# A convolution-attention and feed-forward kernel on one core: a softmax constant moved to ScalarE, the bound of x from a sum of four maxima, and VectorE's side work moved to the ends of groups of four units

## The chip, the core and the metric

The kernel runs on one core of one Trainium2 chip. The metric is the device time of one execution, in microseconds. The engines are TensorE (PE; its weight loads are PEld), VectorE (DVE), ScalarE (ACT), GpSimd (POOL) and SyncE (SP), which issues the DMAs. Each engine works off its own queue in order and waits for the others by semaphores.

## What is computed

```python
# attention: a softmax over K=7 taps weighs 7 shifted copies of x, per head
w = weight_gen - max(weight_gen, axis=-1)          # [4, 4096, 8 heads, 7 taps]
w = exp(w);  w = w / (sum(w, axis=-1) + 1e-9)
y = einsum('bshk,bskhg->bshg', w, windows_of_7(x)) # [4, 4096, 192]
# feed-forward over the 16384 rows of y
h = y @ w_in                                       # 192 -> 2048
g = h * (1 / (1 + exp(-1.702 * h)))
out = g @ w_out                                    # 2048 -> 192, float32
```

## The kernel before

The 16384 rows are cut into 32 **blocks** of 512 rows. Each block has 16 **units**, one for each 128 of the 2048 inner columns, and units are written out in **groups of four** (u0 to u3). So a block has four groups; they are called A, B, C and D here.

One unit: `whole` (L379 to L382) and `halves` (L390, L391, one pair for two units) put h into a PSUM bank, with float16 high and low parts. `gate` is a ScalarE tanh (L396) and a VectorE product (L397). `split` is a ScalarE copy of the high part (L402) and a VectorE residue (L403), the last read of the bank. `second` (L413 to L415) multiplies the parts with w_out, 12 matmuls per unit, one group later.

TensorE's order in a group is: whole u0, 12 second matmuls of an earlier unit, whole u1, the two pairs of halves, 12 seconds, whole u2, 12 seconds, whole u3, 12 seconds. VectorE's order is: gate u0, gate u1, split u0, split u1, gate u2, split u2, gate u3, split u3. The first matmul L390 of a group's halves marks its start on TensorE below.

The h banks come from a pool of five PSUM banks, `ps_h`; a new tile gets the bank that was given back longest ago.

Beside the units runs the preparation of later blocks, one step at a time:

- `softmax` (L129 to L140): VectorE max, GpSimd subtract, ScalarE exp, VectorE sum (L135), VectorE add of 1e-9 (L136), VectorE reciprocal, GpSimd multiply.
- `attend` (L146, L161): GpSimd's seven taps of a block, a multiply and (from the second tap) an add of 768 elements, into a tile `acc`, of which there are two.
- `scales`: a power-of-two scale from the largest |acc| of the block. VectorE: a reduce over acc (L224), a transpose (L198), a reduce (L199) and, against a mask `groups`, a multiply that spreads four partial maxima over four columns (L200). TensorE adds over partitions with a matrix of ones (L203, its result is the tile `top` in one of the five h banks). VectorE takes the largest of four (L205), cuts it to its exponent (L206) and forms the scales (L210 to L212, L233, L238).
- `split_x`: ScalarE (L264) and VectorE (L267, two instructions) cut acc into float16 parts; `turn` transposes them by DMA into `xt` and copies a part into `xd`, which `whole` and `halves` of that block read.

Where these steps stand is set by hand. `plan(slots, generator)` gives each step a time, counted in units, and `until(end)` inside a group lets out all steps that are due. A slot's fraction of a group, 0 to 4, picks the place: below 0.7 between gate u0 and gate u1, below 1.4 between split u0 and split u1, below 2.1 after gate u2, below 3 after gate u3, and from 3 on at the group's end, after split u3. For a block that starts at unit n, before: `scales` at n - 12.6 (end of group A of the block ahead), n - 9.9 and n - 9.7 (group B, after gate u3), `split_x` at n - 8.9 and n - 8.3 (end of group B). The max of a softmax stands at n - 40, its sum at n - 33, the end of a group A.

Of the kernel before, what the change touches and what calls it, by code (L numbers as in the profile page):

```python
# [22 lines left out]
def conv_attention_then_ffn(  # L23
# [100 lines left out]
    def softmax(blk, eng, out=None):  # L124
# [89 lines left out]
    def scales(blk):  # L214
# [241 lines left out]
    with tc.manual_schedule():  # L456
# [54 lines left out]
        plan((8.8, 11.2, 11.7), scales(1))  # L511
        plan((11.8,), scales_gate(1))
        plan((11.9,), scales_out(1))
        plan((12.2, 12.7), split_x(1))
        plan((12.9, 14.1), turn(1))
# [115 lines left out]
```

## Time and profile before

| | before |
|---|---|
| median of 3 runs | 1122.77 us (1122.59 to 1123.49) |
| profiled execution, its time | 1120.45 us |
| its span, first to last instruction | 1118.7 us |
| PE busy | 1062.0 us (95%) |
| DVE busy | 920.8 us (82%) |
| ACT busy | 708.4 us (63%) |
| POOL busy | 711.1 us (64%) |
| mean granted TensorE clock | 0.986 |

The busy shares are means over a start of some 90 us, in which weights are prepared and TensorE waits much, and a long steady part. TensorE is nearest to the span, but matmuls are pipelined, so a busy TensorE is not one at its peak; what matters is how far apart groups start.

### The profile page before, as it was taken

The numbers are of one execution on the slowest core, as the hardware profiler recorded it, in microseconds if no ns is written. First come the engines' busy times: TensorE is split into PE (matmuls) and PEld (weight loads), VectorE is DVE, ScalarE is ACT, GpSimd is POOL, SyncE is SP. The second block draws the span as 40 slices with busy tenths as digits, with TensorE's granted clock in tenths as the row PEclk, the third lists the DMA queues.
The fourth block names the chain that finished last, engine by engine and source line by source line (L and its number), as shares of the span: only waits on it lengthen the run. The fifth ranks groups of instructions, "written<-read, shape, count | busy, mean of one in ns | idle before, by whom it ended". The sixth has DMA issues, their size and how long they took to land.

```text
span 1118.7 us, 22160 instructions
## 1 busy us (share of the span) xinstructions
PE 1062.0 (95%) x8821; PEld 724.8 (65%) x8821; DVE 920.8 (82%) x1656; ACT 708.4 (63%) x1215; POOL 711.1 (64%) x483
## 2 busy tenths in 40 slices
PE   4388999999999999999999999999999999999998
PEld 4155666666666666666666666666666666666666
DVE  9887788888888888888888888888888888888765
ACT  5855666666666666666666666656666666666665
POOL 5346886666687666678666668766667866669200
PEclk8699999999999999999999999999999999999999
DMA  9301210313021021202112121121202102110110
GB/s 314 103 1 46 75 32 17 89 32 87 18 89 32 18 89 32 84 20 70 37 32 89 30 75 32 31 75 32 90 22 82 31 18 89 32 30 17 32 32 15
DMA packets 73231, 60.71 MB, mean 54 GB/s; under 512 B 60588, under 2 KB 65964, under 8 KB 71592
## 3 DMA queue, kind: packets, MB, share of 16 engines
q1 hardware_dynamic: 73128, 59.30, 18.4%
q8 instruction: 69, 1.13, 0.4%
q14 instruction: 34, 0.28, 0.1%
HBM read 31.96 MB, written 12.58 MB: 40 GB/s over the span
## 4 chain that ended last, share of the span: by engine, by line
DVE 57%; ACT 20%; PE 17%; issue 6%; DMA 0%; DVEq 0%; SPq 0%; ACTq 0%
DVE h L397 19%; DVE g L403 17%; ACT g L402 15%; DVE wm L136 4%; DVE tf L200 3%; ACT th L396 3%; PE o L413 3%; DVE xs L267 3%; PE o L415 3%; PE o L414 3%; DVE top L224 2%; PE h L379 2%; PE h L380 2%; PE h L381 2%; PE h L382 2%
## 5 line engine op out<-in xcount | busy, mean ns | idle before, releaser
L402 ACT ACTIVATE g<-h 128x512 f16<-128x512 f32 x512 | 305.2, 596 | 330.7 <-DVE h L397 330.7
L413 PE MATMUL o<-wos,g 128*128 128x192 f16 x2048 | 505.4, 247 | 0.0
L415 PE MATMUL o<-woh,g 128*128 128x192 f16 x2048 | 504.1, 246 | 0.0
L414 PE MATMUL o<-wol,g 128*128 128x192 f16 x2048 | 504.1, 246 | 0.0
L403 DVE SCALAR_TENSOR_TENSOR g<-g,h 128x512 f16<-128x512 f16 x512 | 345.1, 685 | 158.5 <-ACT g L402 147.8
L396 ACT ACTIVATE th<-h,s 128x512 f32<-128x512 f32 x512 | 336.3, 682 | 56.0 <-PE h L391 54.3
L397 DVE SCALAR_TENSOR_TENSOR h<-th,h 128x512 f32<-128x512 f32 x512 | 343.1, 687 | 17.7 <-ACT th L396 17.4
L161 POOL TENSOR_TENSOR acc<-acc,prod 128x768 f32<-128x768 f32 x186 | 337.1, 1813 | 14.6
L146 POOL TENSOR_TENSOR prod<-xb,wb 128x768 f32<-128x768 f32 x186 | 287.6, 1546 | 9.8
L413 PEld LDWEIGHTS <-g 128*128 128x128 f16 x2048 | 200.2, 98 | 102.4 <-issue 57.1
L414 PEld LDWEIGHTS <-g 128*128 128x128 f16 x2048 | 200.5, 98 | 41.1 <-issue 0.3
L379 PE MATMUL h<-xt,w0l 128*128 128x512 f16 x512 | 195.3, 381 | 18.8 <-DVE g L403 13.2
L415 PEld LDWEIGHTS <-g 128*128 128x128 f16 x2048 | 200.5, 98 | 0.0
L380 PE MATMUL h<-xt,w0h 128*128 128x512 f16 x512 | 194.9, 381 | 0.0
L381 PE MATMUL h<-xt,w0h 128*128 128x512 f16 x512 | 194.8, 380 | 0.0
L382 PE MATMUL h<-xt,wth 128*128 128x512 f16 x512 | 194.6, 380 | 0.0
L131 POOL TENSOR_TENSOR wb<-wb,wm 128x224 f32<-128x224 f32 x31 | 17.9, 577 | 263.6 <-DVE wm L129 263.6
L381 PEld LDWEIGHTS <-w0h 128*128 128x128 f16 x512 | 50.3, 98 | 61.0 <-issue 1.1
L382 PEld LDWEIGHTS <-wth 128*128 128x128 f16 x512 | 50.3, 98 | 61.0 <-issue 1.0
L391 PE MATMUL h<-xd,tl 64*128 64x512 f16 x256 | 81.7, 381 | 1.8 <-DVE g L403 1.8
L390 PE MATMUL h<-xt,tl 64*128 64x512 f16 x256 | 77.1, 381 | 0.0
L379 PEld LDWEIGHTS <-w0l 128*128 128x128 f16 x512 | 50.2, 98 | 26.6 <-DVE g L403 19.0
(89 smaller groups left out, 595.3 us busy)
## 6 DMA issues: line engine op xcount, KB each, us to landing
xb<-in_x_dram SPq DMA_DIRECT2D x12, 1344.0 KB, 6.3
out_dram<-osb SPq DMA_DIRECT2D x31, 384.0 KB, 2.4
wb<-in_weight_gen_dram SPq DMA_DIRECT2D x16, 224.0 KB, 3.1
ro<-in_moe_w_out_dram SPq DMA_DIRECT2D x4, 768.0 KB, 12.1
xb<-in_x_dram SPq DMA_DIRECT2D x3, 768.0 KB, 6.3
ri<-in_moe_w_in_dram SPq DMA_DIRECT2D x4, 512.0 KB, 8.3
xb<-in_x_dram SPq DMA_DIRECT2D x4, 504.0 KB, 5.8
xd<-xt SPq DMA_DIRECT2D x31, 64.0 KB, 2.1
```

Of the source, the lines that this page charges most:

```text
L146: eng.tensor_tensor(to.rearrange("p j (h g) -> p (j h) g", g=G), xv, wv, ALU.mult)
L161: nc.gpsimd.tensor_tensor(acc, acc, t, ALU.add)
L379: nc.tensor.matmul(ps, lhsT=w0l[:, s], rhs=x0, start=start, stop=False)
L381: nc.tensor.matmul(ps, lhsT=w0h[:, s], rhs=x0, start=False, stop=False)
L382: nc.tensor.matmul(ps, lhsT=th_[:, s], rhs=x1, start=False, stop=stop)
L396: nc.scalar.activation(t, hp[u], AF.Tanh, scale=scale[u[0]][:, 4:5])
L397: nc.vector.scalar_tensor_tensor(hp[u], t, 1.0, hp[u], ALU.add, ALU.mult)
L402: nc.scalar.activation(g[:, 0], hp[u], AF.Copy, scale=2.0**-12)
L403: nc.vector.scalar_tensor_tensor(g[:, 1], g[:, 0], -(2.0**12), hp.pop(u), ALU.mult, ALU.add)
L413: nc.tensor.matmul(o, lhsT=lo, rhs=wos[:, d], start=a and j % 2 == 0, stop=False, skip_group_check=True)
L414: nc.tensor.matmul(o, lhsT=hi, rhs=wol[:, d], start=False, stop=False, skip_group_check=True)
L415: nc.tensor.matmul(o, lhsT=hi, rhs=woh[:, d], start=False, stop=z, skip_group_check=True)
```

## The change

Three edits.

1. In `softmax`, for blocks 2 and up, the 1e-9 is added by a ScalarE Copy with a bias, in the same step as the sum; the reciprocal becomes a step of its own, later.
2. In `scales`, the second reduce writes straight into the column that goes to TensorE; the multiply with `groups` goes. The matmul with ones then yields the sum of four partial maxima (each of 32 partitions) instead of four maxima, and the reduce over four (L205) goes too; the exponent is cut from PSUM directly. The sum is at most four times the largest. The bounds of the weights keep the old form.
3. The slots move.

```diff
         nc.vector.tensor_reduce(m, w, axis=AX.X, op=ALU.add)
-        nc.vector.tensor_scalar(m, m, 1e-9, None, ALU.add)
+        if blk < XB:
+            nc.vector.tensor_scalar(m, m, 1e-9, None, ALU.add)
+        else:
+            nc.scalar.activation(m, m, AF.Copy, bias=1e-9)
+            yield
         nc.vector.reciprocal(r, m)
...
+        n = 4 if exact else 1
         nc.vector.transpose(a, t)
-        nc.vector.tensor_reduce(m[:, 0:1], a, axis=AX.X, op=ALU.max)
-        nc.vector.tensor_scalar(four, groups, m[:, 0:1], None, ALU.mult)
+        if exact:
+            nc.vector.tensor_reduce(m[:, 0:1], a, axis=AX.X, op=ALU.max)
+            nc.vector.tensor_scalar(four, groups, m[:, 0:1], None, ALU.mult)
+        else:
+            nc.vector.tensor_reduce(four[:, 0:1], a, axis=AX.X, op=ALU.max)
         yield
...
-        nc.vector.tensor_reduce(m[:, 1:2], ps[:, 0:4], axis=AX.X, op=ALU.max)
-        nc.vector.tensor_scalar(e, m[:, 1:2].bitcast(I32), 0x7F800000, None, ALU.bitwise_and)
+        top = ps[:, 0:1]
+        if exact:
+            top = m[:, 1:2]
+            nc.vector.tensor_reduce(top, ps[:, 0:4], axis=AX.X, op=ALU.max)
+        nc.vector.tensor_scalar(e, top.bitcast(I32), 0x7F800000, None, ALU.bitwise_and)
...
-            plan([n - 12.6, n - 9.9, n - 9.7], scales(blk))
+            plan([n - 12.2, n - 10.4, n - 10.3], scales(blk))
-            plan([n - 8.9, n - 8.3], split_x(blk))
+            plan([n - 9.5, n - 8.2], split_x(blk))
```

VectorE, end of a group A and the group B behind it, before (`tf` is the column or columns for TensorE, `ta` the transposed maxima, `wm` and `wr` a softmax's sum and reciprocal):

```order
L403 SCALAR_TENSOR_TENSOR g<-g,h 128x512
L224 TENSOR_REDUCE top_102<-acc 128x1
L198 STREAM_TRANSPOSE ta<-top_102 128x32
L199 TENSOR_REDUCE tm<-ta 128x1
L200 TENSOR_SCALAR tf<-groups,tm 128x4
L397 SCALAR_TENSOR_TENSOR h<-th,h 128x512 x2
L403 SCALAR_TENSOR_TENSOR g<-g,h 128x512 x2
L397 SCALAR_TENSOR_TENSOR h<-th,h 128x512
L403 SCALAR_TENSOR_TENSOR g<-g,h 128x512
L397 SCALAR_TENSOR_TENSOR h<-th,h 128x512
L205 TENSOR_REDUCE tm<-top 128x1
L206 TENSOR_SCALAR s<-tm 128x1
```

The same place after:

```order
L414 SCALAR_TENSOR_TENSOR g<-g,h 128x512
L135 TENSOR_REDUCE wm<-wb 128x32
L235 TENSOR_REDUCE top_103<-acc 128x1
L203 STREAM_TRANSPOSE ta<-top_103 128x32
L208 TENSOR_REDUCE tf<-ta 128x1
L408 SCALAR_TENSOR_TENSOR h<-th,h 128x512 x2
L414 SCALAR_TENSOR_TENSOR g<-g,h 128x512 x2
L408 SCALAR_TENSOR_TENSOR h<-th,h 128x512
L217 TENSOR_SCALAR s<-top 128x1
```

The multiply into `tf` and the reduce of `top` are gone, the sum of a softmax has joined the end of group A, and the scale's instructions stand behind gate u2 where they stood behind gate u3.

TensorE in group B, before (`h_2786` is the bank of u3):

```order
L381 MATMUL h_2786<-xt_2434,w0h_94 128x512
L382 LDWEIGHTS wth_96
L382 MATMUL h_2786<-xt_2434,wth_96 128x512
L203 LDWEIGHTS ones_92
L203 MATMUL top_2847<-tf_2757,ones_92 128x4
L413 LDWEIGHTS g_2750
```

and after (`h_2779` is the bank of u2):

```order
L392 MATMUL h_2779<-xt_2429,w0h_94 128x512
L393 LDWEIGHTS wth_96
L393 MATMUL h_2779<-xt_2429,wth_96 128x512
L211 LDWEIGHTS ones_92
L211 MATMUL top_2819<-tf_2752,ones_92 128x1
L424 LDWEIGHTS g_2719
```

The matmul with ones now stands one unit earlier on TensorE, ahead of 12 seconds and u3's four matmuls.

VectorE in block 0, where block 1 is prepared, before (the two L267 stand in group D behind split u0):

```order
L397 SCALAR_TENSOR_TENSOR h<-th,h 128x512 x2
L403 SCALAR_TENSOR_TENSOR g<-g,h 128x512
L267 SCALAR_TENSOR_TENSOR xs<-acc,s,xs 128x4x128
L267 SCALAR_TENSOR_TENSOR xs<-acc,s,xs 128x4x64
L403 SCALAR_TENSOR_TENSOR g<-g,h 128x512
```

and after (end of group C, ahead of group D's first two gates):

```order
L414 SCALAR_TENSOR_TENSOR g<-g,h 128x512
L135 TENSOR_REDUCE wm<-wb 128x32
L129 TENSOR_REDUCE wm<-wb 128x32
L278 SCALAR_TENSOR_TENSOR xs<-acc,s,xs 128x4x128
L278 SCALAR_TENSOR_TENSOR xs<-acc,s,xs 128x4x64
L408 SCALAR_TENSOR_TENSOR h<-th,h 128x512 x2
```

The DMA that turns block 1 follows the two instructions, so it is issued ahead of group D's gates and no longer behind its split u0. On GpSimd the subtract of a softmax, before between the third and fourth tap of a block, now stands between its fifth and sixth, and waits for a max at the end of a group C (before: in the group C, behind gate u0). The order of SyncE's DMAs is the same.

## Rows read from the trace of the kernel before

**Rows 1.** Windows: stretch, each engine's busy us (instructions), granted clock, DMA share, GB/s

```profile
91.40:188.16 96.76, 96.76 (x821) 66.78 (x821) 77.17 (x145) 63.71 (x108) 70.08 (x48) 1.00 0.16 44
188.16:1049.18 861.02, 847.85 (x7100) 577.31 (x7100) 722.26 (x1273) 547.10 (x935) 595.90 (x393) 1.00 0.18 49
```

**Rows 2.** Timeline of PE, group B of block 6 and C's start: start, us, instruction

```profile
261.86 0.39 PE L390 MATMUL h<-xt,tl 64*128 64x512 f16 x1
...
264.25 0.25 PE L413 MATMUL o<-wos,g 128*128 128x192 f16 x1
...
266.11 0.17 PE L203 MATMUL top<-tf,ones 128*128 128x4 bf16 x1
...
267.81 0.39 PE L379 MATMUL h<-xt,w0l 128*128 128x512 f16 x1 [0.52 <-DVE g L403]
...
270.63 0.39 PE L390 MATMUL h<-xt,tl 64*128 64x512 f16 x1
...
271.03 0.37 PE L391 MATMUL h<-xd,tl 64*128 64x512 f16 x1
```

**Rows 3.** Timeline of DVE over groups A and B of the same block

```profile
256.46 1.26 DVE L397 SCALAR_TENSOR_TENSOR h<-th,h 128x512 f32<-128x512 f32 x2
...
262.91 0.94 DVE L224 TENSOR_REDUCE top<-acc 128x1 f32<-128x768 f32 x1
...
264.36 1.45 DVE L200 TENSOR_SCALAR tf<-groups,tm 128x4 bf16<-128x4 f32 x1
265.72 1.28 DVE L397 SCALAR_TENSOR_TENSOR h<-th,h 128x512 f32<-128x512 f32 x2
267.06 1.29 DVE L403 SCALAR_TENSOR_TENSOR g<-g,h 128x512 f16<-128x512 f16 x2
...
272.61 1.14 DVE L267 SCALAR_TENSOR_TENSOR xs<-acc,s,xs 128x512 f16<-128x512 f32 x2
```

**Rows 4.** Timeline of POOL over the same stretch

```profile
263.97 1.81 POOL L161 TENSOR_TENSOR acc<-acc,prod 128x768 f32<-128x768 f32 x1
274.72 0.57 POOL L131 TENSOR_TENSOR wb<-wb,wm 128x224 f32<-128x224 f32 x1 [8.95 <-DVE wm L129]
```

**Rows 5.** DVE groups by line in 220.69 to 1015.54: busy us, mean ns, idle before

```profile
L136 DVE TENSOR_SCALAR wm<-wm 128x32 f32<-128x32 f32 x24 | 43.2, 1799 | 0.8
L200 DVE TENSOR_SCALAR tf<-groups,tm 128x4 bf16<-128x4 f32 x24 | 34.7, 1446 | 0.9
...
L135 DVE TENSOR_REDUCE wm<-wb 128x32 f32<-128x224 f32 x24 | 9.1, 378 | 0.0
...
L199 DVE TENSOR_REDUCE tm<-ta 128x1 f32<-128x32 f32 x24 | 4.5, 186 | 0.8
```

**Rows 6.** ACT groups by line over the whole span

```profile
L133 ACT ACTIVATE wb<-wb 128x224 f32<-128x224 f32 x32 | 12.2, 382 | 0.7 <-POOL wb L131 0.6 <-DVE wb L131 0.2
...
L325 ACT ACTIVATION_READ_ACCUMULATOR abs<-ro 128x1 f32 x6 | 1.1, 188 | 0.0
```

**Rows 7.** Timelines of POOL, DVE, SP and PE, end of block 0, block 1's start

```profile
75.63 1.81 POOL L161 TENSOR_TENSOR acc<-acc,prod 128x768 f32<-128x768 f32 x1
77.02 0.21 DVE L233 TENSOR_SCALAR s<-s,sc 128x1 f32<-128x1 f32 x1
79.13 1.81 POOL L161 TENSOR_TENSOR acc<-acc,prod 128x768 f32<-128x768 f32 x1
79.58 3.60 DVE L267 SCALAR_TENSOR_TENSOR xs<-acc,s,xs 128x512 f16<-128x512 f32 x2
81.02 1.87 POOL L146 TENSOR_TENSOR prod<-xb,wb 128x768 f32<-128x768 f32 x1
83.24 1.55 SPq L273 DMA_TRANSPOSE xt<-xs  x1
87.03 0.61 PE L379 MATMUL h<-xt,w0l 128*128 128x512 f16 x1 [5.62 <-DMA xt<-xs]
91.40 0.39 PE L390 MATMUL h<-xt,tl 64*128 64x512 f16 x1
92.60 0.69 DVE L397 SCALAR_TENSOR_TENSOR h<-th,h 128x512 f32<-128x512 f32 x1 [3.83 <-ACT th L396]
```

More of the change, by code (lines that the diff above doesn't have):

```diff
@@ L190, in conv_attention_then_ffn, with top_of @@
     to_in, to_out = sc[:, 2:3], sc[:, 3:4]
-    def top_of(t, e):
+    def top_of(t, e, exact):
         a = spool.tile([P, 32], F32, tag="ta", name="ta", bufs=2)
@@ L197, in top_of @@
         four = spool.tile([P, 4], BF16, tag="tf", name="tf", bufs=2)
+        n = 4 if exact else 1
         nc.vector.transpose(a, t)
-        nc.vector.tensor_reduce(m[:, 0:1], a, axis=AX.X, op=ALU.max)
-        nc.vector.tensor_scalar(four, groups, m[:, 0:1], None, ALU.mult)
+        if exact:
[3 more added lines that the diff above has]
+            nc.vector.tensor_reduce(four[:, 0:1], a, axis=AX.X, op=ALU.max)
         yield
         ps = ps_h.tile([P, N], F32, tag="h", name="top")
-        nc.tensor.matmul(ps[:, 0:4], lhsT=ones, rhs=four, start=True, stop=True)
+        nc.tensor.matmul(ps[:, 0:n], lhsT=ones, rhs=four[:, 0:n], start=True, stop=True)
         yield
-        nc.vector.tensor_reduce(m[:, 1:2], ps[:, 0:4], axis=AX.X, op=ALU.max)
-        nc.vector.tensor_scalar(e, m[:, 1:2].bitcast(I32), 0x7F800000, None, ALU.bitwise_and)
+        top = ps[:, 0:1]
[3 more added lines that the diff above has]
+        nc.vector.tensor_scalar(e, top.bitcast(I32), 0x7F800000, None, ALU.bitwise_and)
     def power(e, to, inv, top):
@@ L227, in scales @@
         e = s[:, 0:1].bitcast(I32)
-        yield from top_of(t, e)
+        yield from top_of(t, e, False)
         power(e, s[:, 2:3], s[:, 3:4], 263)
@@ L328, in bound @@
         nc.vector.tensor_reduce(tops[1][:, 0:1], sums[:, a0:a1], axis=AX.X, op=ALU.max)
-        yield from top_of(tops[1], e)
+        yield from top_of(tops[1], e, True)
     def bound_in():
@@ L510, in conv_attention_then_ffn @@
         plan((8.0,), scales_out(0))
[L511 to L515, printed above, removed]
+        plan((8.2, 9.6, 9.7), scales(1))
+        plan((9.75,), scales_gate(1))
+        plan((9.8,), scales_out(1))
+        plan((10.5, 11.8), split_x(1))
+        plan((11.85, 14), turn(1))
         for blk in range(2, NB):
             n = blk * NF
-            plan([n - 12.6, n - 9.9, n - 9.7], scales(blk))
-            plan([n - 9.6], scales_gate(blk))
-            plan([n - 9.5], scales_out(blk))
-            plan([n - 8.9, n - 8.3], split_x(blk))
-            plan([n - 8.2, n - 5.8], turn(blk))
+            plan([n - 12.2, n - 10.4, n - 10.3], scales(blk))
+            plan([n - 10.25], scales_gate(blk))
+            plan([n - 10.2], scales_out(blk))
+            plan([n - 9.5, n - 8.2], split_x(blk))
+            plan([n - 8.15, n - 6], turn(blk))
             if blk == 2:
-                plan((4.8, 4.81, 8.1, 8.8, 9.1), softmax(blk, G_))
+                plan((4.8, 4.81, 8.1, 8.5, 8.8, 9.1), softmax(blk, G_))
                 plan([9.2 + 1.5 * k for k in range(K)], attend(blk))
-            else:
-                plan([n - 40, n - 39.9, n - 35, n - 33, n - 30.4], softmax(blk, G_))
-                first_tap, step = (n - 27.8, 2) if blk == 3 else (n - 30, 2.2)
-                plan([first_tap + step * k for k in range(K)], attend(blk))
+            elif blk == 3:
+                plan((3.7, 7.75, 7.8, 11.7, 13.7, 17.6), softmax(blk, G_))
+                plan([n - 27.8 + 2 * k for k in range(K)], attend(blk))
+            else:
+                plan([n - 52.3, n - 52.2, n - 48.2, n - 44.3, n - 36.3, n - 30.4], softmax(blk, G_))
+                plan([n - 30 + 2.2 * k for k in range(K)], attend(blk))
             if blk % XB == 0 and blk > XB:
```

## The prediction, made before the changed kernel ran

> **What bounds the kernel now.** I read the windows first, cut where blocks start on TensorE. Blocks 1 to 3 take 96.76 us, 32.25 each, and TensorE is busy in all of it at a granted clock of 1.00. The 26 blocks behind them take 861.02 us, 33.12 each, at the same clock and with 13.2 us of idle TensorE [rows 1]. The work is the same, so 32.25 is what TensorE itself needs for a block, 8.06 per group, and 861.02 - 26 x 32.25 = 22.5 us are lost to waits. That is the prize.
>
> Where it goes shows in one block's timeline of TensorE. Group B starts at 261.86, group C at 270.63, 8.77 later, and not 8.06. The row at 267.81 names the wait: the first matmul of C's u0 stood 0.52 us idle until a split (L403) on VectorE. The second halves of C come at 271.03, another 0.15 late [rows 2]. Together this is the 0.87 per block.
>
> Why the split is late: VectorE had finished group A at 262.9, then took 1.45 us for the multiply L200, four columns wide. So gate u0 of B started at 265.72 and its two first splits at 267.06; the first ends 0.69 later, at 267.75, and TensorE goes on at 267.81 [rows 2, 3]. L200 ends at 265.81, when GpSimd's add of a tap ends: 263.97 + 1.81 = 265.78 [rows 4]. It is not computing, it waits for GpSimd. The reduce L199 just ahead (0.19) runs under the same add and does not wait. Over 24 blocks L200 takes 1446 ns every time and the add of 1e-9, L136, 1799, against 186 and 378 for reduces of like size [rows 5].
>
> One thing makes group B the sore one: `top` takes the fifth h bank there, so C's u0 needs the bank of B's u0, four units back and not five.
>
> **The change part by part.**
>
> *The sum of maxima* takes L200 and L205 off VectorE: 1.45 + 0.15 per block. What fills `tf` now is a reduce; I price it as L199, 0.19, which it replaces, so nothing is added.
>
> *The constant on ScalarE* takes 1.80 off VectorE per block [rows 5], but not off the path: group A, in which it sat, shows no loss. The new ScalarE Copy of 32 elements lies between the 188 ns of an accumulator read and the 382 of the exp of 224 elements [rows 6]; I take 0.25. A wait comes with it: on ScalarE the next group's two tanh are queued behind it, and VectorE's gates behind those.
>
> *The moves.* I lay the new order out for a steady block, in us from each group's start on TensorE. The first gate can start 1.2 in (91.40 to 92.60) [rows 7]. From there to the end of split u3 is 6.5 (256.46 to 262.9) [rows 3]. So VectorE's main work of a group ends at 7.7 and the next begins at 8.06 + 1.2 = 9.26: 1.5 us are free at every group's end.
>
> - End of A: sum 0.38 and L224 to L199, 1.45 (262.91 to 264.36) [rows 3, 5]: 1.8. B's first gate is 0.3 late. The ScalarE add ends at 7.7 + 0.38 + 0.25 = 8.35, or 8.5 at the upper price; the tanh behind it needs its halves and cannot start before 9.26 - 0.7 = 8.56. Cost nothing. If VectorE were late here by over 0.2, the tanh would be late by the rest.
> - `tf` is ready at 7.7 + 1.8 = 9.5, 1.45 into B. TensorE now reaches the matmul for `top` behind u2, at 264.25 - 261.86 = 2.39, not at 4.25 [rows 2]. Margin 0.9; what is queued behind it on TensorE is all the rest, so past that margin each us costs one.
> - The six scale instructions, 0.15 to 0.21 each, some 1.0 in all, stand behind gate u2, where VectorE waits some 0.65 for a ScalarE copy anyway: 0.35 late. The same cost stood behind gate u3 before.
> - C's u0 is reached 267.81 - 0.69 - 261.86 = 5.26 into B. B's split u0 now ends at 1.5 + 1.34 + 0.69 = 3.5. Margin 1.7, and the loss of 0.87 is gone.
> - End of B: 1.2 + 0.3 + 6.5 + 0.35 = 8.35, then the two L267, 1.14 when GpSimd is quiet [rows 3]: 9.5, C's first gate 0.25 late. The transposing DMA leaves here, with two groups to land in; it took 3.8 [rows 7].
> - End of C: reciprocal and max, 0.7 of the 1.5 free. End of D: an exp on ScalarE.
>
> So every group should start 8.06 after the last one. **22.5 us** go; the upper end of the remaining loss is among the rivals.
>
> *GpSimd under the new order.* Its subtract waits for the max at the end of C, so a cycle starts some 0.8 behind that. It works 33.12 - 8.95 = 24.2 us of a block, less a short wait of about 0.5 [rows 4], and is done 24.3 to 25 after C's end. Three groups, 24.2, lie between an end of C and the next end of B. So the L267 pair starts just as GpSimd's last add of the cycle ends, maybe under its last 0.1 to 0.8 us. In block 0 such a pair met a busy GpSimd throughout and took 3.60 in place of 1.14 [rows 3, 7]. The page "GPSIMD Engine Reference" of the Trainium skill (Key points) says that GpSimd's SBUF interfaces are shared with VectorE instructions in a 2-port mode or with two SBUF inputs; L267 has two, L200 and L136 would be of the first kind, and the rows agree. By that rule alone the new place of L267 speaks against the change.
>
> *Block 0* has a second prize. The last VectorE part of block 1's x ended at 83.2 there; its transpose was issued at 83.24, and TensorE stood 5.62 us until 87.03 [rows 7]; from there to the halves at 91.40 took 4.37 where 32.25-us blocks need 2.8, 1.56 more. With the pair at the end of C, I put its end near 78.7: three gates and splits sooner, but tanh u1 of C now waits behind the ScalarE add (0.9) and the pair still meets GpSimd. Transposed 3.8 later, at 82.5; TensorE, which now waits some 1.9 for `top` in C, wants it at 82.3. Block 1 could start up to 5.9 sooner. Part goes back at once: block 2's seven taps begin at some 72 as before, take 24.5 with two softmax steps between (seven taps at 3.5, 79.13 - 75.63), and end near 96.5, but block 1's end of A would now be at 93. VectorE stands till 96.5 in its reduce, TensorE till 98.2 for `top`, where it would have been at 101.85 before: 3.65 sooner. Two collisions of L267 with GpSimd in blocks 1 and 2 take some 0.8. Net **2.8**, bounds 0 and 5.9. Ahead of block 0 the same two VectorE instructions go once: 0 to 1.5 (an L200 and an L205), I take **0.5**, as ScalarE and DMAs bound part of that stretch.
>
> Sum: 22.5 + 2.8 + 0.5 = 25.8. The profiled execution took 1120.45, 1.75 more than its span of 1118.7; it would become 1094.7. The median lies 2.3 above that execution, so 1122.8 - 25.8 = **1097.0**.
>
> **The rivals.**
>
> 1. *L267 collides in full in each block* (pair 3.6 or more). C's first gate starts 8.35 + 3.6 - 8.06 = 3.9 into C, its split u2 ends 4.6 later at 8.5, and D's second halves want that bank at 8.28: 0.2 lost per block. If both instructions met a fresh add, 4.5: 1.1 lost. Over 27 blocks 5 to 30 us back; mid 13, so 1110, at most 1122 or so. For it: GpSimd's end falls on the pair's start. Against: behind that add GpSimd has nothing to do for 8 us, so only the rest of one instruction can be in the way.
> 2. *The new reduce into `tf` waits for GpSimd as L200 did* (1.25 more). `tf` is then ready 2.7 into B, TensorE stands 0.3 per block: some 8 us back, 1105. Against: L199 never waited.
> 3. *The scale's small instructions wait*, slower than before. They ran while GpSimd was idle; after gate u2 of B its taps run. L210 to L212, L233 and L238 are scalar operations on SBUF as L200 is, five in a row, each of which could wait for an instruction of 1.54 to 1.81. Split u2 of B would end at 6.5 + d, and C wants its bank at 8.28. For d = 2.6 (two of five meet one) 0.85 is lost per block and the gain is gone; from there on it is slower: for d = 4.3, 2.5 lost, 27 x 2.5 = 68 us back, 1165. Against: at 77.02 L233 took 0.21 under the add that ran from 75.63 to 77.44 [rows 7], with the others around it. "VectorE: DVE Perf Modes" of the Trainium skill (the perf-mode tier table) lets tensor_scalar on float32 in SBUF use both ports, with no word on one element; that page would have them wait, and the row says no.
> 4. *The banks were not what held TensorE* and the loss comes back elsewhere: 1120 to 1125. Against: blocks 1 to 3 run at 32.25.
>
> **How the numbers follow.** Forecast 0.67, rival 1 0.15 (most of it faster, 0.02 at no change), rival 2 and other partial gains 0.07, rival 3 0.07, rival 4 0.04. About 0.2%, 2.2 us, can be told from no change. Faster 0.87, the same 0.06, slower 0.07. The range runs from 22.5 + 5.9 + 1.5 with a little of the spread of runs, 1092, up into the milder half of rival 1, 1110.
>
> **What would show it.** Groups start 8.06 apart in all blocks from 2 on, and TensorE has no idle time there for L403. L200 and L136 are gone, save for the start, and nothing on VectorE takes 1.4 us for a few elements. The L267 pair takes 1.1 to 1.9. The ScalarE add takes about 0.25 and no tanh waits for it in steady blocks. TensorE's wait for `xt` in block 0 shrinks to under 2 us, and a wait for `top` of about 2 us appears in blocks 0 and 1. Wrong if the matmul for `top` waits in every block, or if L210 to L238 grow.

## The result and the profile after

The changed kernel takes 1094.91 us (median of 4 runs, 1093.89 to 1095.54) beside 1122.68 us (1121.38 to 1123.49) before, a ratio of 0.9753 with an interval of 0.9736 to 0.977. The forecast was 1097.0 with a range of 1092 to 1110. The profiled execution took 1095.54 us with a span of 1093.6; the span of before was 1118.7, so 25.1 us of it are gone.

In the new code all lines lie further down: the halves are L401 and L402, tanh L407, gate L408, ScalarE copy L413, split L414, seconds L424 to L426, the matmul for `top` L211, the reduces into it L235 and L208, the scale's instructions L217 to L249, the two `split_x` instructions L278, the new ScalarE add L139.

The windows, cut at starts of blocks on TensorE as in [rows 1] (stretch, its length, each engine's busy us and instructions, granted clock, DMA share, GB/s): blocks 2 and 3, and the 26 blocks behind them.

```profile
120.96:185.47 64.51, 64.51 (x548) 44.53 (x548) 51.75 (x93) 43.37 (x76) 50.82 (x33) 1.00 0.18 53
185.47:1024.12 838.65, 838.65 (x7100) 578.70 (x7100) 640.74 (x1192) 558.75 (x959) 592.93 (x392) 1.00 0.18 51
```

The same 26 blocks took 861.02 us before; they now take 838.65, 32.25 or 32.26 each but for one of 32.32, and TensorE is idle in none of it. That is 22.37 us. Block 2 starts at 120.96 where it started at 123.65, 2.69 sooner. 22.37 + 2.69 = 25.06 is the whole difference of the spans.

TensorE in group B of a steady block, and the start of C, as in [rows 2]:

```profile
258.03 0.39 PE L401 MATMUL h<-xt,tl 64*128 64x512 f16 x1
...
260.43 0.17 PE L211 MATMUL top<-tf,ones 128*128 128x1 bf16 x1
...
263.30 0.38 PE L390 MATMUL h<-xt,w0l 128*128 128x512 f16 x1
...
266.11 0.39 PE L401 MATMUL h<-xt,tl 64*128 64x512 f16 x1
```

Group B is 8.08 long instead of 8.77. The matmul for `top` waits for nothing, and C's first `whole` at 263.30, 5.27 into the group, has no wait beside it; in [rows 2] it came 5.95 in and stood for a split.

VectorE over the same stretch, as in [rows 3]; a bracket gives the idle time ahead and what ended it:

```profile
251.18 1.29 DVE L408 SCALAR_TENSOR_TENSOR h<-th,h 128x512 f32<-128x512 f32 x2 [1.50 <-ACT th L407]
...
257.66 0.38 DVE L135 TENSOR_REDUCE wm<-wb 128x32 f32<-128x224 f32 x1
...
259.18 0.19 DVE L208 TENSOR_REDUCE tf<-ta 128x1 bf16<-128x32 f32 x1
259.28 1.28 DVE L408 SCALAR_TENSOR_TENSOR h<-th,h 128x512 f32<-128x512 f32 x2
...
262.43 0.15 DVE L217 TENSOR_SCALAR s<-top 128x1 int32<-128x1 int32 x1
...
263.31 0.20 DVE L249 TENSOR_SCALAR s<-s,sc 128x1 f32<-128x1 f32 x1
...
265.98 1.14 DVE L278 SCALAR_TENSOR_TENSOR xs<-acc,s,xs 128x512 f16<-128x512 f32 x2
267.32 1.29 DVE L408 SCALAR_TENSOR_TENSOR h<-th,h 128x512 f32<-128x512 f32 x2 [0.20 <-ACT th L407]
...
275.38 1.29 DVE L408 SCALAR_TENSOR_TENSOR h<-th,h 128x512 f32<-128x512 f32 x2 [0.99 <-ACT th L407]
```

and GpSimd's timeline and ScalarE's beside it:

```profile
262.38 1.55 POOL L150 TENSOR_TENSOR prod<-xb,wb 128x768 f32<-128x768 f32 x1
264.00 1.81 POOL L165 TENSOR_TENSOR acc<-acc,prod 128x768 f32<-128x768 f32 x1
```

```profile
258.07 0.23 ACT L139 ACTIVATE wm<-wm 128x32 f32<-128x32 f32 x1 [1.05 <-DVE wm L135]
258.52 1.27 ACT L407 ACTIVATE th<-h,s 128x512 f32<-128x512 f32 x2 [0.22 <-PE h L402]
```

What to see: VectorE now waits for a tanh ahead of the first gates of C, D and A (0.20, 0.99, 1.50), 2.69 us per block. The tanh waits for TensorE's halves. Over the whole span "ScalarE's tanh waits for TensorE's halves" has grown from 54.3 to 128.8 us, and "VectorE's gate waits for the tanh" from 17.4 to 82.9. The small instructions L217 to L249 take 0.15 to 0.21 while GpSimd multiplies a tap (262.38 to 263.93), and the L278 pair starts at 265.98, 0.17 behind the end of GpSimd's last add (264.00 + 1.81).

The plainest sign is the part of the page on the chain of work that ended last (shares of the span). Before:

```profile
DVE 57%; ACT 20%; PE 17%; issue 6%; DMA 0%; DVEq 0%; SPq 0%; ACTq 0%
```

and after:

```profile
PE 92%; DVE 3%; POOL 2%; ACT 2%; issue 1%; DMA 0%; POOLq 0%; ACTq 0%
```

Before, the end hung on VectorE and ScalarE; now it hangs on TensorE. The prediction did not use that line. It should have, as the experiments show.

### The profile page after: what moved, and what is told of

Its sections match the earlier page's. It is cut to its first block, busy times and chain, and to the rows that moved or that the text cites. A ratio compares the mean times of both kernels' runs of the same rounds, so it can differ in the third digit from the quotient of the medians.

```text
span 1093.6 us, 22203 instructions
## 1 busy us (share of the span) xinstructions
PE 1053.7 (96%) x8821; PEld 726.0 (66%) x8821; DVE 834.6 (76%) x1562; ACT 721.3 (66%) x1245; POOL 711.2 (65%) x483
## 4 chain that ended last, share of the span: by engine, by line
PE 92%; DVE 3%; POOL 2%; ACT 2%; issue 1%; DMA 0%; POOLq 0%; ACTq 0%
PE o L424 16%; PE o L426 15%; PE o L425 15%; PE h L391 10%; PE h L392 10%; PE h L390 10%; PE h L393 10%; PE h L401 6%; POOL acc L165 1%; POOL prod L150 1%; PE tr L183 1%; DVE h L408 1%; ACT abs L336 1%; DVE g L414 0%; ACT bits L326 0%
## 5 line engine op out<-in xcount | busy, mean ns | idle before, releaser
L424 PE MATMUL o<-wos,g 128*128 128x192 f16 x2048 | 504.9, 247 | 0.0
L426 PE MATMUL o<-woh,g 128*128 128x192 f16 x2048 | 503.7, 246 | 0.0
L414 DVE SCALAR_TENSOR_TENSOR g<-g,h 128x512 f16<-128x512 f16 x512 | 340.1, 684 | 155.3 <-ACT g L413 147.0
L413 ACT ACTIVATE g<-h 128x512 f16<-128x512 f32 x512 | 305.7, 597 | 190.8 <-DVE h L408 190.7
L407 ACT ACTIVATE th<-h,s 128x512 f32<-128x512 f32 x512 | 337.0, 683 | 128.8 <-PE h L402 128.8
L408 DVE SCALAR_TENSOR_TENSOR h<-th,h 128x512 f32<-128x512 f32 x512 | 341.8, 690 | 82.9 <-ACT th L407 82.9
L424 PEld LDWEIGHTS <-g 128*128 128x128 f16 x2048 | 200.0, 98 | 97.6 <-issue 53.0
L426 PEld LDWEIGHTS <-g 128*128 128x128 f16 x2048 | 200.3, 98 | 0.0
L402 PE MATMUL h<-xd,tl 64*128 64x512 f16 x256 | 77.7, 383 | 1.0 <-DVE g L414 1.0
L401 PE MATMUL h<-xt,tl 64*128 64x512 f16 x256 | 77.4, 383 | 0.0
```

The source lines that it names most:

```text
L407: nc.scalar.activation(t, hp[u], AF.Tanh, scale=scale[u[0]][:, 4:5])
L408: nc.vector.scalar_tensor_tensor(hp[u], t, 1.0, hp[u], ALU.add, ALU.mult)
L413: nc.scalar.activation(g[:, 0], hp[u], AF.Copy, scale=2.0**-12)
L414: nc.vector.scalar_tensor_tensor(g[:, 1], g[:, 0], -(2.0**12), hp.pop(u), ALU.mult, ALU.add)
L424: nc.tensor.matmul(o, lhsT=lo, rhs=wos[:, d], start=a and j % 2 == 0, stop=False, skip_group_check=True)
L426: nc.tensor.matmul(o, lhsT=hi, rhs=woh[:, d], start=False, stop=z, skip_group_check=True)
```

## The experiments

Each time stands beside runs of the kernel before on the same chip.

**One half of the change alone.** The first kernel is the one of before with the sum of four maxima only (no L200, no L205), all slots and the constant as they were:

```diff
-        nc.vector.tensor_reduce(m[:, 0:1], a, axis=AX.X, op=ALU.max)
-        nc.vector.tensor_scalar(four, groups, m[:, 0:1], None, ALU.mult)
+        if exact:
+            nc.vector.tensor_reduce(m[:, 0:1], a, axis=AX.X, op=ALU.max)
+            nc.vector.tensor_scalar(four, groups, m[:, 0:1], None, ALU.mult)
+        else:
+            nc.vector.tensor_reduce(four[:, 0:1], a, axis=AX.X, op=ALU.max)
...
```

> The kernel before with the sum of four maxima alone; L136 and all slots as before. Theory (two waits of VectorE for GpSimd, at the add of 1e-9 and at the multiply into tf, add up to 2.7 us of lateness of group B's first gate, against a bank margin of 1.7 us, so either one removed is enough): gate u0 of B starts about 2.5 us into B, its first split ends at 4.5, C's first matmul is reached at 5.26, no wait; steady blocks take 32.25 us and not 33.12, block 0 stays as it was: about 1100 us. Rival (the lateness is only pushed along, each us of VectorE costs): about half the loss stays, 1108 to 1112.

The second is the one of before with the constant on ScalarE only:

```diff
-        nc.vector.tensor_scalar(m, m, 1e-9, None, ALU.add)
+        if blk < XB:
+            nc.vector.tensor_scalar(m, m, 1e-9, None, ALU.add)
+        else:
+            nc.scalar.activation(m, m, AF.Copy, bias=1e-9)
+            yield
...
-                plan([n - 40, n - 39.9, n - 35, n - 33, n - 30.4], softmax(blk, G_))
+                plan([n - 40, n - 39.9, n - 35, n - 33, n - 32.9, n - 30.4], softmax(blk, G_))
```

> The kernel before with the constant on ScalarE alone; the multiply into tf and all slots as before, the reciprocal right behind the sum. Theory: the wait of 1.4 us at the end of group D goes, so A ends sooner and B's first gate starts 1.5 to 2.0 us into B although the multiply still waits for GpSimd: no wait at C, 32.25 us per block, about 1100 us. Rival (the prediction's reading, the add is off the path and only the multiply counts): no change, 1121 to 1123 us.

Measured: 1098.92 us, ratio 0.979 (0.9776 to 0.9805), and 1100.55 us, ratio 0.9806 (0.9792 to 0.9821). A window over 26 blocks from the start of block 2, first of the one, then of the other:

```profile
123.27:961.86 838.59, 838.59 (x7101) 578.46 (x7100) 656.82 (x1223) 550.88 (x936) 597.24 (x396) 1.00 0.19 53
```

```profile
126.15:964.74 838.59, 838.59 (x7100) 578.40 (x7100) 670.26 (x1249) 557.10 (x962) 596.76 (x396) 1.00 0.19 53
```

Both are at 32.25 us per block: **either half alone brings all of the steady blocks' gain.** The two do not add. This falls on the prediction's sentence that the 1.80 of L136 is "off the path"; had that been so, the second kernel would have stayed at 33.12. And the wait of the instruction that was kept shrinks as well. In the first kernel's window L136 takes 485 ns, in the second's the multiply into `tf` (there L204) takes 1034, against 1799 and 1446 in [rows 5] (groups of VectorE by line: busy us, mean ns, idle before):

```profile
L136 DVE TENSOR_SCALAR wm<-wm 128x32 f32<-128x32 f32 x26 | 12.6, 485 | 0.9
```

```profile
L204 DVE TENSOR_SCALAR tf<-groups,tm 128x4 bf16<-128x4 f32 x26 | 26.9, 1034 | 0.9
```

The price of waiting out a GpSimd instruction is in most rows what is left of it when VectorE arrives, and this shifts when anything else does: in the second kernel the same multiply takes from 0.23 to 1.64 us from one block to the next.

**The bank.** The prediction named the bank that `top` takes in `ps_h` as what makes group B sore. This kernel is the one of before with `top` in another PSUM pool from block 2 on:

```diff
-        ps = ps_h.tile([P, N], F32, tag="h", name="top")
+        ps = ps_o.tile([P, N], F32, tag="o", name="top") if other else ps_h.tile([P, N], F32, tag="h", name="top")
...
```

> The kernel before with one edit: from block 2 on, top takes a bank of the other PSUM pool, the one of the output sums, so the five h banks are not shifted in group B. All VectorE work and its waits stay. Theory (C's u0 waits because top has taken the fifth bank and it needs the bank of B's u0): C's u0 no longer waits though L200 still takes 1.4 us; only C's second halves may wait 0.2: 1101 to 1106 us. Rival (VectorE's lateness holds TensorE whatever the banks): 1121 to 1123 us.

Measured: 1122.07 us, ratio 0.9997 (0.9988 to 1.0007), no change. TensorE's starts of groups A, B and C of a block (D begins at 278.38, the next A at 286.63):

```profile
253.51 0.39 PE L390 MATMUL h<-xt,tl 64*128 64x512 f16 x1
...
261.57 0.39 PE L390 MATMUL h<-xt,tl 64*128 64x512 f16 x1
...
269.95 0.39 PE L390 MATMUL h<-xt,tl 64*128 64x512 f16 x1
```

The groups take 8.06, 8.38, 8.43 and 8.25 where they took 8.06, 8.77, 8.22 and 8.06. The sore group is gone, and the sum stays: 33.12 either way. The 26 blocks of [rows 1] in this kernel,

```profile
188.28:1049.11 860.83, 859.29 (x7100) 578.87 (x7100) 721.68 (x1273) 544.98 (x935) 595.62 (x393) 1.00 0.18 49
```

take as long as the 861.02 of before, and TensorE is busy in all but 1.54 of it, where it was idle for 13.2. So its busy time did not tell that it was held back; the spacing of groups did. The bank only chose the place at which the loss was seen. This theory fell.

**What takes its place: VectorE's own chain.** VectorE's gates and splits of a group, with the ScalarE copies in between, take 6.48 us if nothing else comes (251.18 to 257.66 above), 25.92 per block. In the kernel before, the side work came on top with no time to spare. The end of a group D in VectorE's timeline:

```profile
253.95 0.38 DVE L135 TENSOR_REDUCE wm<-wb 128x32 f32<-128x224 f32 x1
254.36 1.79 DVE L136 TENSOR_SCALAR wm<-wm 128x32 f32<-128x32 f32 x1
256.19 0.35 DVE L137 RECIPROCAL wr<-wm 128x32 f32<-128x32 f32 x1
```

From 253.95 to A's gates at 256.46 [rows 3] are 2.51 us. (The text ahead of the prediction puts this sum at the end of a group A; the rows show it at the end of a group D, one group earlier.) The end of A, 262.91 to 265.72 [rows 3], is 2.81. The L267 pair takes 1.06 (272.61 to 273.67), and the other ends of groups in this block are these:

```profile
273.67 0.69 DVE L397 SCALAR_TENSOR_TENSOR h<-th,h 128x512 f32<-128x512 f32 x1
...
280.43 1.29 DVE L397 SCALAR_TENSOR_TENSOR h<-th,h 128x512 f32<-128x512 f32 x2
...
287.06 0.38 DVE L135 TENSOR_REDUCE wm<-wb 128x32 f32<-128x224 f32 x1
```

So the gates and splits take 6.45 in A, 6.89 in B, among them the scale's instructions, 6.76 in C, among them the max, and 6.63 in D. 2.51 + 6.45 + 2.81 + 6.89 + 1.06 + 6.76 + 6.63 = 33.11, the 33.12 of a block. That the pieces of a timeline add up to its period would hold for any engine; what matters is which waits are in them. VectorE's groups by line over the 24 blocks of [rows 5] (busy us, mean ns, idle before and what ended it):

```profile
L403 DVE SCALAR_TENSOR_TENSOR g<-g,h 128x512 f16<-128x512 f16 x385 | 259.9, 685 | 120.5 <-ACT g L402 112.0
L397 DVE SCALAR_TENSOR_TENSOR h<-th,h 128x512 f32<-128x512 f32 x384 | 257.1, 686 | 0.0
```

VectorE waited for ScalarE's copies of its own products, and no gate waited for a tanh; TensorE waited for VectorE, through whichever bank came late first. The trace of before holds one more sign of this. At the start of blocks 1, 2 and 3, where TensorE lost nothing, L136 took 0.36, 0.49 and 0.72 us, and L200 in them 0.23, 0.61 and 1.44, so at most 2.16 together. From block 5 on they took 1.80 and 1.45, 3.25 together, and TensorE lost 0.87: up to 2.38 would have fitted.

After the change the same sum is 25.92 + 1.62 (257.66 to 259.28) + 0.22 + 1.14 + 0.59 = 29.5, and 32.25 - 29.5 = 2.75 is, to 0.06, the 2.69 of waits seen above. This can be tested: side work that fits into 2.69 us must cost nothing, and more must cost the difference. So reduces that nobody reads were put at the end of every group C of the changed kernel, two in one kernel and four (`range(4)`) in the other:

```diff
+        idle = spool.tile([P, 1], F32, tag="idle", name="idle", bufs=1)
+        def extra():
+            for _ in range(2):
+                nc.vector.tensor_reduce(idle, woh[:, 0:768], axis=AX.X, op=ALU.max)
+        for blk in range(2, NB):
+            plan([blk * NF - 4.1], once(extra))
```

> The changed kernel, and at the end of every group C from block 1 on two more VectorE reductions of 768 elements to a tile that nobody reads, at the price of the 768-element reduction of the changed kernel (0.94 us) 1.9 us per block. Theory (VectorE's chain of a block bounds it): the chain of the changed kernel is 29.6 of the 32.25 us that TensorE takes, idle 0.20, 0.99 and 1.50 us ahead of three of the four pairs of gates; 1.9 us fits, block stays 32.25, total 1094 to 1097. Rival (a place near the group's start is what matters, whatever the block's sum): each block loses at that place 1.9 less the 0.99 that stands behind it, some 0.9 us, 23 us in all: 1116 to 1120.

> The changed kernel, and at the end of every group C from block 1 on four more VectorE reductions of 768 elements, 3.8 us per block. Theory: the chain becomes 29.6 + 3.8 = 33.4 us, 1.1 us over TensorE's 32.25; over 26 blocks 29 us, total 1118 to 1128, TensorE idle at the starts of groups, and the last chain of waits mostly on VectorE again as in the kernel before. Rival (a place near the group's start is what matters): the loss is 3.8 less 0.99 at that place, some 2.8 us per block, 73 us: 1160 to 1170.

Measured with two: 1096.17 us, ratio 0.9759 (0.9743 to 0.9775), steady blocks at 32.25; only blocks 2, 3, 28 and 29 took more, 32.40 to 32.83. The interval overlaps that of the changed kernel nearly in full. With four: 1130.21 us, ratio 1.0065 (1.0044 to 1.0086). The chain and a window over 23 steady blocks with four:

```profile
DVE 58%; ACT 21%; PE 11%; issue 7%; POOL 2%; DMA 0%; ACTq 0%; POOLq 0%
```

```profile
240.03:1007.35 767.32, 756.28 (x6281) 510.14 (x6281) 643.55 (x1150) 489.51 (x852) 524.53 (x348) 1.00 0.18 50
```

767.32 / 23 = 33.36 per block; the four reduces took 3.90 together, 3.80 of it until the next instruction could start, and 32.25 - 2.69 + 3.80 is 33.36. The total missed its range by 2 us on the high side: 1.11 x 26 is the 29 us that were expected, and blocks 1 and 2 lost more than that, 2.1 us in block 1, whose group D took 10.12, and 3.1 in block 2 beyond its 1.11. The chain's shares are close to those of the kernel before. This is the strongest run of the study: the slack read from three brackets of one timeline gave the price of a load to a tenth of a microsecond per block.

**The second limit: `top` stands in TensorE's queue.** Here the change's slots are kept and one or both old computations put back. Both first:

```diff
-        if blk < XB:
-            nc.vector.tensor_scalar(m, m, 1e-9, None, ALU.add)
-        else:
-            nc.scalar.activation(m, m, AF.Copy, bias=1e-9)
+        nc.vector.tensor_scalar(m, m, 1e-9, None, ALU.add)
+        if blk >= XB:
             yield
...
-        if exact:
-            nc.vector.tensor_reduce(m[:, 0:1], a, axis=AX.X, op=ALU.max)
-            nc.vector.tensor_scalar(four, groups, m[:, 0:1], None, ALU.mult)
-        else:
-            nc.vector.tensor_reduce(four[:, 0:1], a, axis=AX.X, op=ALU.max)
+        nc.vector.tensor_reduce(m[:, 0:1], a, axis=AX.X, op=ALU.max)
+        nc.vector.tensor_scalar(four, groups, m[:, 0:1], None, ALU.mult)
...
```

> The changed kernel with both old computations put back (add of 1e-9 and multiply into tf on VectorE, reduce of four): only the slots are new. Theory: both waits for GpSimd now fall on the end of group A, one behind the other, so tf is ready 3.5 to 4.5 us into B while TensorE reaches the matmul for top 2.4 us in and stands 1 to 2 us in each block: 25 to 55 us over the changed kernel, 1120 to 1150 us. Rival (the moves are what freed the time): 1095 to 1100 us.

Measured: 1127.49 us (1124.91 to 1130.87), ratio 1.0058 (1.0038 to 1.0078), slower than before by 0.6%: the slots without the two edits lose. TensorE's timeline in a group B, and VectorE's groups by line over 21 steady blocks (698.62 us, 33.27 each):

```profile
267.49 0.18 PE L205 MATMUL top<-tf,ones 128*128 128x4 bf16 x1 [0.75 <-DVE tf L202]
```

```profile
L136 DVE TENSOR_SCALAR wm<-wm 128x32 f32<-128x32 f32 x21 | 33.7, 1607 | 0.7
...
L202 DVE TENSOR_SCALAR tf<-groups,tm 128x4 bf16<-128x4 f32 x21 | 7.1, 338 | 0.8
```

Now L136 stands at the end of A and waits out the add, and the multiply behind it, L202, finds GpSimd between two instructions in 19 of the 21 blocks: 0.25 us there and 1.17 in the other two, 0.34 in the mean, instead of 1.45. By the sum of VectorE's chain (29.5 + 1.61 + 0.34 + 0.19 for the reduce of four) 31.6 would fit into 32.25. It doesn't help, since `tf` comes late: group B takes 9.0, the others 8.06. In the changed kernel `tf` is ready at 259.37 and TensorE reaches the matmul at 260.43, a margin of 1.06; L136 and L202 put 1.95 in front of it, 0.9 too much.

The constant alone put back,

```diff
-        if blk < XB:
-            nc.vector.tensor_scalar(m, m, 1e-9, None, ALU.add)
-        else:
-            nc.scalar.activation(m, m, AF.Copy, bias=1e-9)
+        nc.vector.tensor_scalar(m, m, 1e-9, None, ALU.add)
+        if blk >= XB:
             yield
```

> The changed kernel with the add of 1e-9 back on VectorE, in the step of the sum at the end of group A. Theory (with the first four runs: VectorE's and ScalarE's chain of one block took 33.1 us and bounded the kernel before; the new order has room there, but TensorE stands for top whenever tf is later than 2.4 us into B): the add starts about 258.0 in the traced block and waits for GpSimd's add to end at 258.8, so tf is ready about 2.2 us into B, at the edge: 0 to 0.4 us lost per block, 1095 to 1106 us. Rival (the ScalarE add is what gained): 1110 us or more.

and the old maxima alone put back (the second piece of the diff above),

> The changed kernel with the old maxima: the multiply into tf and the reduce of four back on VectorE, the constant on ScalarE, the new slots. Theory: the multiply starts 1.35 us into B and waits for a GpSimd instruction that ends 2.4 into B, so TensorE stands 0 to 0.4 us per block for top: 1095 to 1106 us. Rival (the sum of maxima is what gained): 1110 us or more.

give 1106.88 us (1105.12 to 1108.14), ratio 0.986 (0.9844 to 0.9876), 0.9 us beyond its range, and 1105.02 us, ratio 0.9845 (0.9829 to 0.9862). In the first of them, over 22 steady blocks:

```profile
266.67:987.96 721.29, 713.41 (x6007) 487.82 (x6007) 569.14 (x1034) 468.54 (x793) 501.08 (x333) 1.00 0.18 50
```

32.79 per block in the mean. One block of them takes 34.36, with an L136 of 3.90 that ends behind two further GpSimd instructions; nearly all others take 32.71, with an L136 of 1.42: 1.42 - 1.06 = 0.36 against 0.46 measured. "TensorE's `top` waits for VectorE's `tf`" comes 26 times. In the second the multiply takes 0.28 and 1.2 us in turn, and 2.1 to 2.6 in three blocks; a steady group B takes 8.08 or 8.3 with it, 9.2 to 9.7 in those three, and the one of block 1 takes 13.46. So in the old slots either edit was enough, and **in the new slots both are needed for the full gain**: the new slots have moved the limit from VectorE's sum to one date, `tf` at 2.4 us into group B.

**What the slots bring.** Both new computations in the kernel of before, with its old slots (the diffs of the first two kernels together):

> The constant on ScalarE and the sum of maxima, all slots as before (the reciprocal right behind the sum). Theory: steady blocks at 32.25 us, nothing more than either of the two alone gives, since TensorE bounds then; block 0 as before with its wait of 5.6 us for the transposed x: 1098 to 1101 us. Rival (the two gains add up): 1080 us or less.

and the changed kernel with block 1's slots alone set back:

```diff
-        plan((8.2, 9.6, 9.7), scales(1))
+        plan((8.8, 11.2, 11.7), scales(1))
...
-        plan((10.5, 11.8), split_x(1))
-        plan((11.85, 14), turn(1))
+        plan((12.2, 12.7), split_x(1))
+        plan((12.9, 14.1), turn(1))
```

> The changed kernel with block 1's preparation at its old slots; all else new. Theory: steady blocks as in the changed kernel, but block 0 waits about 5.6 us for the transposed x again and block 1 no longer about 2 us for top: block 2 starts 2.5 to 3 us later, 1097 to 1099 us. Rival (the start's difference is the granted clock or the spread of runs): 1094 to 1096 us.

Measured: 1097.89 us, ratio 0.9782 (0.9768 to 0.9797), and 1099.15 us, ratio 0.9791 (0.9776 to 0.9806). Each total lies 0.1 to 0.2 us beyond its range, the first below, the second above. Steady blocks take 32.25 in both. Block 2 starts at 123.15 in the one, at 124.76 in the other, and at 120.96 in the changed kernel. So the slots of the steady blocks bring nothing, and those of block 1 bring some 2 to 4 us, once; the first interval still touches that of the changed kernel, the second does not.

**Two tries at the start.** What is left to gain lies in blocks 0 and 1. In the changed kernel, TensorE waits in block 0 for `top` and for block 1's transposed x, and in block 1 for `top` (timeline of TensorE; compare the 5.62 in [rows 7]):

```profile
70.24 0.18 PE L211 MATMUL top<-tf,ones 128*128 128x1 bf16 x1 [1.64 <-DVE tf L208]
83.77 0.39 PE L390 MATMUL h<-xt,w0l 128*128 128x512 f16 x1 [0.46 <-DMA xt<-xs]
99.16 0.18 PE L211 MATMUL top<-tf,ones 128*128 128x1 bf16 x1 [1.94 <-DVE tf L208]
```

The first try plans block 2's softmax and taps much sooner:

```diff
-        if blk < XB:
+        if blk <= XB:
             nc.vector.tensor_scalar(m, m, 1e-9, None, ALU.add)
...
-        plan((8.2, 9.6, 9.7), scales(1))
+        plan((7.9, 9.6, 9.7), scales(1))
...
-        plan((10.5, 11.8), split_x(1))
-        plan((11.85, 14), turn(1))
+        plan((10.5, 11.6), split_x(1))
+        plan((11.65, 14), turn(1))
...
-                plan((4.8, 4.81, 8.1, 8.5, 8.8, 9.1), softmax(blk, G_))
-                plan([9.2 + 1.5 * k for k in range(K)], attend(blk))
+                plan((3.6, 3.65, 4.81, 5.3, 5.5), softmax(blk, G_))
+                plan((5.6, 7.0, 8.4, 9.8, 12.2, 13.2, 14.2), attend(blk))
...
-                plan((3.7, 7.75, 7.8, 11.7, 13.7, 17.6), softmax(blk, G_))
+                plan((3.7, 3.75, 7.8, 11.7, 13.7, 17.6), softmax(blk, G_))
```

> The changed kernel with only its first blocks planned otherwise: block 1's scales, x parts and transposes a little sooner in block 0, block 2's softmax and attention some five units sooner, block 2's constant on VectorE. In the changed kernel block 1 begins at 86.60 us and its group B then waits about two microseconds for the number that the sum of block 2's attention gives. Theory (VectorE's chain bounds a block, and what is left over the steady blocks is in the order of the first two): block 1 begins near 85.3, its group B no longer waits, and the total falls by 2 to 4 us, to about 1091.5 (1090 to 1093). Rival: the sooner work lies in the same gaps of VectorE and the transposing DMA lands no sooner, so block 0 gives back what block 1 gains: 1094 to 1096.

Measured: 1099.01 us, ratio 0.9786 (0.9771 to 0.9802), slower than the changed kernel. Block 1 no longer waits (32.25), but begins at 91.69 in place of 86.60. VectorE's timeline in block 0, where it still converts w_out (L359, L377), and GpSimd's beside it:

```profile
60.61 0.74 DVE L359 SCALAR_TENSOR_TENSOR wol<-ro,sc,woh 128x512 f16<-128x512 f32 x1
61.27 0.29 DVE L377 TENSOR_SCALAR wos<-woh 128x512 f16<-128x512 f16 x1
...
63.51 1.83 DVE L359 SCALAR_TENSOR_TENSOR wol<-ro,sc,woh 128x512 f16<-128x512 f32 x1
65.27 1.63 DVE L377 TENSOR_SCALAR wos<-woh 128x512 f16<-128x512 f16 x1
```

```profile
63.26 1.54 POOL L150 TENSOR_TENSOR acc<-xb,wb 128x768 f32<-128x768 f32 x1
64.76 1.99 POOL L150 TENSOR_TENSOR prod<-xb,wb 128x768 f32<-128x768 f32 x1
66.82 1.81 POOL L165 TENSOR_TENSOR acc<-acc,prod 128x768 f32<-128x768 f32 x1
```

The conversions, 0.74 and 0.29 while GpSimd is idle, now take up to 1.83 and 1.63. L359 ends 0.54 behind the tap instruction that it meets (65.34 and 64.80), L377 0.15 behind the next (66.90 and 66.75), which itself takes 1.99 in place of 1.54. TensorE waited 4.10 for a split and 3.62 for `top`. Neither the theory nor the rival of this run had named that.

The second try leaves the taps behind the last conversion, and only takes block 2's constant back to VectorE, with its reciprocal directly behind:

```diff
-        if blk < XB:
+        if blk <= XB:
             nc.vector.tensor_scalar(m, m, 1e-9, None, ALU.add)
...
-                plan((4.8, 4.81, 8.1, 8.5, 8.8, 9.1), softmax(blk, G_))
-                plan([9.2 + 1.5 * k for k in range(K)], attend(blk))
+                plan((4.8, 4.81, 8.1, 8.5, 8.6), softmax(blk, G_))
+                plan([8.7 + 1.5 * k for k in range(K)], attend(blk))
...
-                plan((3.7, 7.75, 7.8, 11.7, 13.7, 17.6), softmax(blk, G_))
+                plan((3.7, 7.75, 7.8, 11.7, 13.7, 18.3), softmax(blk, G_))
```

> The changed kernel with only block 2's attention a little sooner, after the last conversion of w_out: block 2's constant on VectorE, its reciprocal directly behind, its GpSimd steps half a unit sooner, and block 3's scaling of the weights behind block 2's last add on GpSimd. Theory (what the changed kernel still loses in block 1 is the wait of TensorE for the sum of block 2's attention, 1.94 us, because GpSimd ends that attention at 97.60 us, and the sooner attempt failed because its GpSimd work lay over VectorE's conversions of w_out): GpSimd ends about 95.2, the wait of 1.94 us is gone, block 2 begins 1 to 2 us sooner, total 1093 to 1094. Rival: the sooner GpSimd work or the two more instructions ahead of a gate in block 0 hold VectorE as long as they save: 1094.5 to 1096.

Measured: 1094.25 us (1093.01 to 1094.59), ratio 0.9748 (0.9734 to 0.9761), between the theory's range and the rival's. Block 1 takes 32.25, the wait of 1.94 is gone, and block 2 starts at 119.21, 1.75 sooner than in the changed kernel; 0.64 of that is an earlier first start. Part went back in block 0, which takes 42.94 in place of 41.94, to the collision that the prediction had feared for every block (timeline of VectorE):

```profile
77.02 3.26 DVE L278 SCALAR_TENSOR_TENSOR xs<-acc,s,xs 128x512 f16<-128x512 f32 x2
```

3.26 in place of 1.80 in the changed kernel's block 0. The interval overlaps the changed kernel's in most of its width, so this version is not shown to be better.

## Why the prediction was right, and where it was not

*The size of the steady gain: right.* 22.5 was forecast and 22.37 came, because the yardstick, blocks 1 to 3 at 32.25, was the true time of TensorE. Why these blocks escaped was not asked: TensorE's work in them is the same, but VectorE's is shorter, as L136 and L200 above show.

*The reason given for it: wrong in two steps.* "Off the path" for L136 and the bank of `top` as what makes group B sore both fell (constant alone; other bank). The prediction looked for the one wait that TensorE showed and followed it one step back, to L200. That wait was only where a long chain on VectorE first touched TensorE. Rival 4, that the banks did not hold TensorE, was right in its premise and wrong in its result: the loss would indeed have come back elsewhere had the edits not shortened VectorE's sum. They did, by 3.6 where 0.87 was enough, so the number came out for another reason than the one written down. With the bank theory alone a reader would have expected the constant to bring nothing.

*`tf` and the margin: right.* Forecast 0.9, measured 1.06 by the timeline, and the kernels with old computations in new slots lose just what goes past it.

*Rival 1: its collision came, and cost next to nothing.* In the block shown the L278 pair starts 0.17 behind GpSimd's last add and takes 1.14, as it does in 20 of the 26 steady blocks. In five it takes 1.45 to 2.60, and in block 28 it runs among GpSimd's taps (timeline of VectorE):

```profile
975.56 3.89 DVE L278 SCALAR_TENSOR_TENSOR xs<-acc,s,xs 128x512 f16<-128x512 f32 x2
```

This is more than the 3.6 of the rival. Yet group C behind the pair takes 8.06 every time, and block 28 takes 32.32 in place of 32.25: the slack took it up, and 3.89 - 1.14 - 2.69 = 0.06 is left. The rival had priced such a pair at 0.2 us and more per block.

*Rivals 2 and 3: not seen in steady blocks.* The reduce into `tf` takes 0.19 in every block, and the scale's instructions do not wait. For the last, the prediction had set a row against a page of the Trainium skill, and the row held: L244 and L249, tensor_scalar on one float32 of SBUF per partition, an operation that "VectorE: DVE Perf Modes" (the perf-mode tier table) lists at twice the base rate, took 0.21 and 0.20 under a GpSimd multiply. The table has no word on one element, so the rows add to it and do not contradict it.

*ScalarE's add: right.* 0.25 was taken, the row says 0.23, and the tanh behind it waits for TensorE, not for it.

*Blocks 0 and 1: near in sum, partly by offsetting errors.* Forecast 2.8 + 0.5, measured 2.69. Block 1 started 4.80 sooner, and gave 2.11 back at block 1's `top`, against "some 3.65 sooner" net of 0.8. The two waits for `top` of about 2 us are there (1.64 and 1.94), and the wait for `xt` shrank to 0.46. The "1.56 more" that the prediction counted behind the old wait was the clock: from 87.03 to 91.40 TensorE was busy throughout at a mean granted clock of 0.64, after 5.62 us of idle; in the changed kernel, after 0.46, the same work from 83.77 to 86.60 took 2.83 at 1.00. The 0.5 ahead of block 0 failed: VectorE was some 0.5 sooner (43.32 for the last conversion ahead of block 0, 43.80 before), TensorE's first `whole` too (41.39 for 41.86), but the halves came 0.68 later, at 44.65 for 43.97. The windows of that stretch, after and then before:

```profile
41.39:43.10 1.71, 1.71 (x6) 0.59 (x5) 1.71 (x3) 1.06 (x3) 0.35 (x2) 0.50 0.45 103
43.10:44.65 1.55, 1.55 (x5) 0.44 (x4) 0.88 (x2) 0.00 (x0) 1.47 (x2) 0.62 0.43 98
```

```profile
41.86:43.01 1.15, 1.15 (x6) 0.50 (x4) 1.15 (x2) 1.07 (x3) 0.00 (x0) 0.75 0.41 95
43.01:43.97 0.96, 0.96 (x6) 0.30 (x5) 0.93 (x3) 0.00 (x0) 0.75 (x2) 1.00 0.46 108
```

The granted clock was 0.50, the lower of the two levels (1.2 GHz), then 0.62 in the mean, against 0.75 and 1.00: the work came sooner, and the clock rose later (windows of 1 us show 0.50 up to 44 after, up to 42 before). This is one execution of each kernel; whether the change moved the clock is not shown. With the kernels of this study, the first halves begin between 43.19 and 45.58 us.

*The total.* The span fell by 25.1 us against 25.8 forecast. The median came out 2.1 below the forecast mainly because the profiled execution of before lay 2.3 under its median, and that was carried over; the changed kernel's profiled execution, 1095.54, lay at the top of its runs.

## What to carry to other kernels

Before blaming a bank or a wait, add up each engine's own work per period, with its waits for its helpers, and compare it with the period. If an engine's sum equals the period and holds no wait for the engine that is seen waiting, its sum is the bound; here the part of the page on the chain of work that ended last said the same. Edits that shorten such a sum do not add: the first 0.87 us here paid 22 us, and the rest became slack, which the brackets ahead of that engine's instructions price for the next change. A small instruction that is seen waiting out another engine's work has no fixed price: the add of 1e-9 took 0.48 us in one order here and 1.80 in another, and moving it ahead of a date such as `tf` can turn slack into a wait.

## What the hardware showed unexpectedly

VectorE instructions of three kinds did not end before GpSimd's instruction in progress. A multiply or add with a constant of 4 or 32 elements (1.45 and 1.80 us, 0.23 and 0.18 with GpSimd idle) ended within 0.03 of it: L200 at 265.81, the tap at 265.78 [rows 3, 4]. A float16 scaling of 512 elements (1.63 for 0.29) ended 0.15 behind it. Products with two inputs outside PSUM (L359 1.83 for 0.74, the L267 or L278 pair up to 3.89 for 1.14) ended further behind it, L359 by 0.54, and the GpSimd instruction that followed was longer in its turn, 1.99 for 1.54. The page "GPSIMD Engine Reference" of the Trainium skill (Key points) describes such sharing for 2-port modes and for two SBUF inputs, and these rows agree. In the kernels before and after, reduces, the transpose, gates and splits with one input from PSUM, and operations of one element per partition did not wait: over all blocks the reduce over `acc` took 0.94 to 0.95, a gate 0.67 to 0.70, a split 0.63 to 0.69.
